# The 64 left-over rows of q and k, padded to 128 partitions and taken third in a batch, in an attention and channel-mix kernel

## The chip, the cores and the metric

The kernel runs on one core of one Trainium2 chip. The metric is the device time of one execution in microseconds (us), as the median of several runs.

## The reference

q, k and v have the shape (4, 6208, 256): four batches of N = 6208 rows with C = 256 columns. Each column of q and k is normalized over the rows, and the attention runs between columns:

```python
qn = q / (np.linalg.norm(q, axis=1, keepdims=True) + 1e-06)
kn = k / (np.linalg.norm(k, axis=1, keepdims=True) + 1e-06)
s = kn.transpose(0, 2, 1) @ qn / tau          # 256 x 256 a batch
a = softmax(s, -1)
x = v @ a                                     # 6208 x 256 a batch
```

A channel mix follows, with x_prev the row before: `xk = mu_k*x + (1-mu_k)*x_prev`, `xr` likewise with mu_r, then `relu(xk @ w_k)**2 @ w_v`, times the sigmoid of `xr @ w_r`. w_k is 256x1024, w_v 1024x256, w_r 256x256. All inputs and the output are fp32.

## The kernel before

**Tiling.** A batch's 6208 rows are NB = 12 groups of 512 and L = 64 left over. For q and k a group of 512 is a tile of 128 partitions with S = 4 rows each; the 64 left-over rows are group NB, on 64 partitions with one row each (`src`, L274). For v the tiles of 512 rows are the blocks of the main pipeline; the left-over rows of all four batches make one more block, "left", run second to last.

**Batch 0 first.** The loop at L335 loads all of batch 0's q and k (two tiles by SyncE's queue, the others by POOL's, which casts fp32 to bf16 on the way), squares them, sums the squares over the rows by matmuls with a column of ones (L376), and accumulates k^T q in PSUM, in `s_ps` (L387). `softmax(0, KC)` turns that into A[0], a 256x256 matrix in bf16 (L480). TensorE's idle time in this phase is filled with matmuls of ones (L841).

**The main pipeline.** For each block of 512 rows: `x_stage` multiplies the turned v with A (L536) and ScalarE copies the result out (L542); `mix_stage` builds xk and xr on VectorE (L576 to L599); `up_stage` multiplies with w_k (L628), with a relu on ScalarE (L632) and a square on VectorE (L634), in four pairs a block; `down_stage` multiplies with w_r (L686, the gate, tanh at L697) and w_v (L693), and VectorE joins both (L699). v is turned by TensorE for the first five blocks (L421) and by DMA transposes on SyncE's queue behind them (L409).

**Batches 1 to 3 of q and k** are worked through beside the blocks of the batch ahead. `qk_load` (L748) issues a group's two loads on POOL's queue into a ring `qk` of NG = 13 buffers; each group of a batch, the one of 64 rows too, takes the next buffer, and batch 1 begins with buffer 0, which batch 0 has used. A load's `gate` makes it wait for a pair of `up_stage`, so that loads are paced; `after_pair` (L884) names the pair, and for times ahead of the first pair it names none, so that batch 1's first two loads wait only for the buffer and for the power that `softmax(0)` takes on POOL (`root0`).

`cov_group` (L757) does a group: ScalarE squares it (L769), VectorE adds the four rows of a partition (L772, L775, in bf16) and carries the sum in fp32 in `far` (L779, L782), and TensorE adds its part of k^T q to `s_ps` (L792). With group 11 the squares in `far` are summed over the partitions by fp32 matmuls with ones (L802) into `acc` (L807). The group of 64 rows is the last of its batch: its two covariance matmuls contract over 64 partitions, its squares go into four matmuls of their own over 64 partitions (L802 again), and L809 adds the result to `acc`. Then `softmax(b)`: POOL raises the norms to the power 0.5 (L287), VectorE makes reciprocals and splits them in three bf16 terms (L289 to L308), TensorE spreads them over the partitions (L314), VectorE scales (L459), ScalarE takes exp (L473), and VectorE writes A[b] (L480).

**What sets the order.** Nothing is issued where it stands in the code. `add` notes each step with its engine, an estimated cost, its key (a due time in units of T = 9.6 us for one block) and what it reads and writes; `Plan.order` (L63) lists the steps by a model of the engines, the ready step with the smallest key first, and the program is written out in that order. Each engine runs its part in order. A step that gets another key, another cost or another buffer can so move others. The keys of a batch's groups are spaced evenly over a span (L869 to L879):

```python
span = (ends[b] - start) / 48.5
for g in range(NB + 1):
    at = start + g * S * span
    cov_group(b, g, at, span)
    need.append((at, "qk", b, g))
```

Of the kernel before, what the change touches and what calls it, by code (L numbers as in the profile page):

```python
# [174 lines left out]
def kernel(  # L175
# [17 lines left out]
    P = 128  # L193
# [14 lines left out]
    def sbuf(name, shape, dt=BF16):  # L208
        return sb.tile([P] + shape, dt, name=name)
# [125 lines left out]
    for i, (tn, g, j0, j1) in enumerate(order0):  # L335
# [43 lines left out]
        if tn == "k":  # L379
            jq = 0  # L380
            for j in range(j0, j1):
                first = "cov" not in seen
                seen.add("cov")

                def go(G=G, g=g, j=j, rows=rows, first=first):
                    for ih in range(2):
                        nc.tensor.matmul(s_ps[:, ih, :], G[:rows, 1, j, ih * P:(ih + 1) * P], G[:rows, 0, j],  # L387
                                         start=first and ih == 0, stop=False, skip_group_check=True)
                add("PE", pe(C, 2), key + .1, go, reads=[buf, ("qk", g, 0, jq)], writes=[("s_ps",)], name="cov0")
# [49 lines left out]
    LEFT = NBLK - 2  # L439


    root0 = []

    def softmax(b, key):
        i = b % 2
# [31 lines left out]
        for ih in range(2):  # L477
            add("DVE", TINY, key + .15 + .01 * ih, lambda ih=ih: nc.vector.reciprocal(sm[i][:, ih:ih + 1], sm[i][:, ih:ih + 1]),
                reads=[("sm", i, ih)], writes=[("sm", i, ih)], name="chain")
            add("DVE", dve(C, 1.4), key + .155 + .01 * ih, lambda ih=ih: nc.vector.tensor_scalar_mul(  # L480
                A[b][:, ih], e_sb[i][:, ih], sm[i][:, ih:ih + 1]), reads=[("e", i, ih), ("sm", i, ih)],
                writes=[("A", b, ih)], name="chain A")

    units = []

# [257 lines left out]
        unit(kl, both)  # L743


    ng, nl = [NB + 1], [NB + 1]

    def qk_load(b, g, key, pace):  # L748
        rows, n = (P, S) if g < NB else (L, 1)
        gi = nl[0] % NG  # L750
        nl[0] += 1
        G = qk[gi]
        for x, t in enumerate((q, k)):
            add("POOL", 0.55, key + x * .001, lambda x=x, t=t: nc.gpsimd.dma_start(G[:rows, x, :n], src(t, b, g)),  # L754
                writes=[("qk", gi, x, j) for j in range(S)], size=rows * n * C * 4, name="ld qk", after=root0, gate=pace(x))

    def cov_group(b, g, key, dk):  # L757
        rows, n = (P, S) if g < NB else (L, 1)

        def work():  # L760
            gi = ng[0] % NG
            si = ng[0] % 2
            ng[0] += 1
            G = qk[gi]
            Q = sq[si]
            both = [("qk", gi, 0, 0), ("qk", gi, 1, 0)]
            sqs = [("sq", si, 0), ("sq", si, 1)]
            w = n * 2 * C
            add("ACT", act(w), key, lambda: nc.scalar.activation(Q[:rows, :, :n], G[:rows, :, :n], AF.Square), reads=both,  # L769
                writes=sqs, name="sq")  # L770
            if n == S:
# [5 lines left out]
                F, fres = far[b % 2], ("far", b % 2)  # L777
                if g == 1:
                    add("DVE", dve(2 * C), key + .25, lambda: nc.vector.tensor_tensor(F, t2[1 - si], t2[si], op=OP.add),  # L779
                        reads=[("t2", 0), ("t2", 1)], writes=[fres], name="carry")  # L780
                elif g > 1:
                    add("DVE", dve(2 * C), key + .25, lambda: nc.vector.tensor_tensor(F, F, t2[si], op=OP.add),  # L782
                        reads=[("t2", si), fres], writes=[fres], name="carry")
                W, wres = F.rearrange("p x c -> p (x c)"), [fres]
                cols = [W[:, x * P:(x + 1) * P] for x in range(4)]
            else:
                wres = sqs
                cols = [Q[:rows, x // 2, 0, (x % 2) * P:(x % 2 + 1) * P] for x in range(4)]
            for s in range(n):
                def go(s=s):  # L790
                    for ih in range(2):
                        nc.tensor.matmul(s_ps[:, ih, :], G[:rows, 1, s, ih * P:(ih + 1) * P], G[:rows, 0, s, :],  # L792
                                         start=g == 0 and s == 0 and ih == 0, stop=g == NB and ih == 1, skip_group_check=True)
# [4 lines left out]
            one = ones_f if n == S else ones  # L798

            def go():  # L800
                for x in range(4):
                    nc.tensor.matmul(xp[:, x:x + 1], cols[x], one[:rows, 0:1], start=x == 0, stop=x == 3,  # L802
                                     skip_group_check=True)
            m_ = add("PE", (0.9, 1.05) if n == S else (0.114, 0.28), kn, go, reads=wres, take="xp", name="norm")
            ai = b % 2
            if g == NB - 1:
                add("DVE", TINY, kn - 3 * T, lambda: nc.vector.tensor_copy(acc[ai], xp[:, 0:4]), after=[m_], give="xp", writes=[("acc", ai)], name="norm")  # L807
            else:
                add("DVE", TINY, kn - 3 * T, lambda: nc.vector.tensor_tensor(acc[ai], acc[ai], xp[:, 0:4], op=OP.add),  # L809
                    after=[m_], give="xp", writes=[("acc", ai)], name="norm")  # L810
        unit(key, work)


# [136 lines left out]
```

## Time and profile before

| | |
|---|---|
| runs | 506.69, 506.70, 508.86 us; median 506.7 |
| profiled execution, its own time | 506.87 us |
| its span from first to last instruction | 505.0 us |
| granted TensorE clock | 1.000 |
| TensorE busy (matmuls) | 486.1 us, 96% |
| VectorE busy | 424.5 us, 84% |
| ScalarE busy | 408.0 us, 81% |
| POOL busy | 102.7 us, 20% |

The profile is of one execution, and the trace's times start with its first instruction. PE is TensorE's matmuls, PEld its weight loads, DVE VectorE, ACT ScalarE, POOL GpSimd, SP SyncE; L792 is line 792 of the kernel that was profiled. Matmuls are pipelined: the trace gives a start and a modelled end that reaches past the start of the next one, so that gaps between them show in the starts. Some matmul records are missing in a trace, so that a count can be one short. A row of the time line merges instructions of one line that follow each other: start, length, engine, line, operation, out<-in, shapes and count.

### The profile page before, as it was taken

Reading aid. Unit: us, or ns where it says so; the run is one execution under the profiler, and the core shown is the slowest. Engines: PE = TensorE matmul, PEld = TensorE weight load, DVE = VectorE, ACT = ScalarE, POOL = GpSimd, SP = SyncE. Lnnn points to the kernel's source line nnn. Section 1 sums busy time; section 2 is a strip of 40 time slices with the busy share of each in tenths; the row PEclk is TensorE's granted clock in tenths of the full one; section 3 lists DMA queues with packets and bytes.
Section 4 is the critical chain, followed back from the end, with each engine's and each line's share of the span. In section 5 each row is a group of like instructions: output and inputs, shape, how many; then the busy total and the mean of one; then the engine's idle time right before and its main releaser. Section 6 shows DMA issues by size and latency. Waiting matters only on the chain.

```text
span 505.0 us, 9492 instructions
## 1 busy us (share of the span) xinstructions
PE 486.1 (96%) x3477; PEld 357.3 (71%) x3536; DVE 424.5 (84%) x979; ACT 408.0 (81%) x582; POOL 102.7 (20%) x174
## 2 busy tenths in 40 slices
PE   2999999999999999999999999999999999999997
PEld 0366777777777777777776777777777777777785
DVE  4569899999899989998879999899779787878974
ACT  6867998898889888888789888888767777777774
POOL 6552222223231211222121122211110111000000
PEclk9999999999999999999999999999999999999999
DMA  9999999999999999999897999995654786542113
GB/s 209 209 205 202 152 135 162 177 228 169 214 180 143 200 180 213 180 157 179 137 176 123 185 175 160 185 169 98 142 109 84 136 123 127 103 105 63 53 75 105
DMA packets 96294, 77.36 MB, mean 153 GB/s; under 512 B 49588, under 2 KB 77944, under 8 KB 96248
## 3 DMA queue, kind: packets, MB, share of 16 engines
q0 software_dynamic: 41776, 38.84, 56.2%
q1 hardware_dynamic: 54472, 37.92, 37.5%
q8 instruction: 27, 0.44, 0.3%
q14 instruction: 19, 0.16, 0.1%
HBM read 78.71 MB, written 25.43 MB: 206 GB/s over the span
## 4 chain that ended last, share of the span: by engine, by line
PE 86%; DMA 6%; DVE 5%; issue 2%; ACT 0%; POOL 0%; DVEq 0%; ACTq 0%; POOLq 0%
PE vr L693 32%; PE kT L628 30%; PE xp L536 8%; PE vr L686 8%; PE s_ps L792 6%; DMA qk<-in_q_dram 3%; DMA v_bf<-in_v_dram 2%; DMA qk<-in_k_dram 2%; DVE kk L634 1%; DVE dl L576 1%; DVE dm L590 1%; PE kT L841 0%; ACT kr L632 0%; DVE xk L599 0%; DVE res L699 0%
## 5 line engine op out<-in xcount | busy, mean ns | idle before, releaser
L632 ACT ACTIVATE kr<-kT 128x1024 bf16<-128x1024 f32 (+1 forms) x200 | 199.7, 1001 | 51.8 <-PE kT L628 45.9
L628 PE MATMUL kT<-xk,w_k 128*128 128x512 bf16 (+1 forms) x742 | 201.2, 372 | 2.8
L693 PE MATMUL vr<-w_v,kk 128*128 128x256 bf16 x1536 | 202.2, 273 | 0.1
L634 DVE TENSOR_TENSOR kk<-kr 128x1024 bf16<-128x1024 bf16 (+1 forms) x200 | 134.1, 671 | 45.3 <-ACT kr L632 45.1
L693 PEld LDWEIGHTS <-kk 128*128 128x128 bf16 x1552 | 169.1, 112 | 3.8 <-DVE kk L634 0.4
L628 PEld LDWEIGHTS <-w_k 128*128 128x128 bf16 x800 | 77.6, 98 | 51.6 <-issue 1.5
L697 ACT ACTIVATE res<-vr 128x256 f32<-128x256 f32 x192 | 74.4, 388 | 12.2 <-PE vr L693 8.5
L699 DVE SCALAR_TENSOR_TENSOR res<-res,vr 128x256 f32<-128x256 f32 x192 | 79.4, 414 | 2.9 <-ACT res L697 2.7
L686 PE MATMUL vr<-w_r,xr 128*128 128x256 bf16 x384 | 73.4, 273 | 0.0
L769 ACT ACTIVATE sq<-qk 128x2048 bf16<-128x2048 bf16 (+1 forms) x39 | 70.6, 1811 | 2.1 <-DMA qk<-in_k_dram 1.4
L542 ACT CAST xR<-xp 128x512 bf16<-128x512 f32 x94 | 55.3, 588 | 13.5 <-PE xp L536 12.7
L403 POOL DMA_DIRECT2D v_bf<-in_v_dram x48 | 36.2, 754 | 146.1 <-PE kT L628 139.1
L686 PEld LDWEIGHTS <-xr 128*128 128x128 bf16 x384 | 42.7, 112 | 30.3 <-issue 0.2
L590 DVE TENSOR_SCALAR dm<-dl,mu 128x512 bf16<-128x512 bf16 (+1 forms) x192 | 59.0, 346 | 0.4
L536 PE MATMUL xp<-vT,A 128*128 128x512 bf16 x188 | 55.9, 379 | 0.5
L792 PE MATMUL s_ps<-qk 128*128 128x256 bf16 (+1 forms) x294 | 55.0, 273 | 0.1
L754 POOL DMA_DIRECT2D qk<-in_q_dram x39 | 20.8, 533 | 97.5 <-ACT res L697 32.4
L792 PEld LDWEIGHTS <-qk 128*128 128x128 bf16 (+1 forms) x294 | 28.5, 98 | 14.6 <-issue 0.6
L576 DVE TENSOR_TENSOR dl<-xR 128x1024 bf16<-128x1024 bf16 (+1 forms) x49 | 33.1, 676 | 0.8 <-ACT xR L542 0.6
L754 POOL DMA_DIRECT2D qk<-in_k_dram x39 | 20.8, 533 | 62.9 <-PE kT L628 42.1
L599 DVE TENSOR_TENSOR xk<-dm,xR 128x1024 bf16<-128x1024 bf16 x47 | 32.5, 691 | 0.9
L599 DVE TENSOR_TENSOR xr<-dm,xR 128x1024 bf16<-128x1024 bf16 x47 | 32.3, 687 | 0.4
(94 smaller groups left out, 259.1 us busy)
## 6 DMA issues: line engine op xcount, KB each, us to landing
out_dram<-res SPq DMA_DIRECT2D x47, 512.0 KB, 4.9
v_bf<-in_v_dram POOLq DMA_DIRECT2D x48, 256.0 KB, 6.8
qk<-in_k_dram POOLq DMA_DIRECT2D x47, 256.0 KB, 7.9
qk<-in_q_dram POOLq DMA_DIRECT2D x46, 256.0 KB, 7.7
res<-in_q_dram SPq DMA_DIRECT2D x2, 512.0 KB, 4.3
vT<-v_bf SPq DMA_TRANSPOSE x43, 7.5
w_k<-in_moe_w_k_dram POOLq DMA_DIRECT2D x1, 512.0 KB, 9.5
w_v<-in_moe_w_v_dram POOLq DMA_DIRECT2D x1, 512.0 KB, 9.5
```

What stands on the lines that cost most here:

```text
L536: nc.tensor.matmul(xp, A[b][:, ih, dh * P:(dh + 1) * P], vT[o].rearrange("p (s h) q -> p h s q", h=2)[:, ih], start=ih == 0, stop=ih == 1)
L590: unit(km, lambda col=col, dh=dh, c0=c0, c1=c1, km=km, w=w: add("DVE", dve(w, 2.77), km, lambda: nc.vector.tensor_scalar_mul(dm[di][:, dh, ...
L599: nc.vector.tensor_tensor(o[which][:, :, c0:c1], dm[di][:, :, c0:c1], xR[:, :, at + c0:at + c1], op=OP.add)
L628: last = nc.tensor.matmul(kT[bk][:, x, :w], w_k[:, dh, fh * P:(fh + 1) * P], xk[n % 2][:, dh, c0:c1], start=dh == 0, stop=dh == 1)
L632: add("ACT", act(2 * w), ku + .1, lambda: nc.scalar.activation(kr[kri][:, :, :w], kT[bk][:, :, :w], AF.Relu, scale=0.5 ** 0.5), reads=[("k ...
L634: add("DVE", dve(2 * w, 2), ku + .2, lambda: nc.vector.tensor_tensor(kk[n % 2][:, 2 * p:2 * p + 2, c0:c1], kr[kri][:, :, :w], kr[kri][:, : ...
L686: nc.tensor.matmul(V[:, D:], tokens(xr[ri][:, dh]), w_r[:, dh, :], start=dh == 0, stop=dh == 1)
L693: nc.tensor.matmul(V[:, :D], tokens(kk[n % 2][:, fh]), w_v[:, fh, :], start=fh == 0, stop=fh == 7)
L697: add("ACT", act(D), kd + .3, lambda: nc.scalar.activation(r[:, s], V[:, D:], AF.Tanh, scale=0.5), reads=[bank], writes=[("res", oi, s)], ...
L699: add("DVE", dve(D), kd + .4, lambda: nc.vector.scalar_tensor_tensor(r[:, s], r[:, s], 1.0, V[:, :D], op0=OP.add, op1=OP.mult), reads=[ban ...
L769: add("ACT", act(w), key, lambda: nc.scalar.activation(Q[:rows, :, :n], G[:rows, :, :n], AF.Square), reads=both, writes=sqs, name="sq")
L792: nc.tensor.matmul(s_ps[:, ih, :], G[:rows, 1, s, ih * P:(ih + 1) * P], G[:rows, 0, s, :], start=g == 0 and s == 0 and ih == 0, stop=g == ...
```

## The change

- The 64 left-over rows get a buffer of their own, `qkl`, with 128 partitions, whose upper 64 partitions are set to zero once, on POOL, in the head. In batches 1 to 3 their covariance matmuls contract over all 128 partitions. In batch 0 `qkl` is used too, but there the operations still take 64 partitions.
- They no longer take a buffer of the ring: a batch takes twelve, and batch 1 begins with buffer 12, which batch 0 leaves unused.
- Their squares go to `sql` on ScalarE, and VectorE adds these in fp32 to the lower 64 partitions of `far`. The four matmuls over 64 partitions and the addition to `acc` (L809) are gone; the fp32 norm matmuls cover all rows of the batch.
- In a batch the 64 rows come third, behind groups 0 and 1, in place of last. The keys' spacing goes from 1/48.5 of the batch's span to 1/49.
- A load for which `after_pair` found no pair now waits for the last VectorE step of A[0].

Lines of the changed kernel are shifted: L792 becomes L793, L802 L803, L807 L805, L536 L540, L628 L632, L693 L697; the new addition is L788.

```diff
+    qkl = sbuf("qkl", [2, 1, C])
+    sql = sbuf("sql", [2, C])
...
-        G = qk[g]
-        buf = ("qk", g, x, j0)
+        G = qk[g] if g < NB else qkl
+        buf = ("qk", g, x, j0) if g < NB else ("qkl", x)
...
+            if b == 0:
+                am.append(a_)
...
-    ng, nl = [NB + 1], [NB + 1]
+    ng, nl = [NB], [NB]
+    add("POOL", 0.4, HK + 6, lambda: nc.gpsimd.memset(qkl[L:], 0.0), writes=[("qkl0",)], name="zero")
...
-        nl[0] += 1
-        G = qk[gi]
+        nl[0] += g < NB
+        G = qk[gi] if g < NB else qkl
...
             else:
-                wres = sqs
-                cols = [Q[:rows, x // 2, 0, (x % 2) * P:(x % 2 + 1) * P] for x in range(4)]
+                G, both = qkl, [("qkl", 0), ("qkl", 1), ("qkl0",)]
+                add("ACT", act(2 * C), key, lambda: nc.scalar.activation(sql[:L], qkl[:L, :, 0], AF.Square), reads=both, writes=[("sql",)], name="sq")
+                add("DVE", dve(2 * C), key + .25, lambda: nc.vector.tensor_tensor(F[:L], F[:L], sql[:L], op=OP.add),
+                    reads=[("sql",), fres], writes=[fres], name="carry")
             for s in range(n):
                 def go(s=s):
                     for ih in range(2):
-                        nc.tensor.matmul(s_ps[:, ih, :], G[:rows, 1, s, ih * P:(ih + 1) * P], G[:rows, 0, s, :],
-                                         start=g == 0 and s == 0 and ih == 0, stop=g == NB and ih == 1, skip_group_check=True)
+                        nc.tensor.matmul(s_ps[:, ih, :], G[:, 1, s, ih * P:(ih + 1) * P], G[:, 0, s, :],
+                                         start=g == 0 and s == 0 and ih == 0, stop=g == NB - 1 and s == S - 1 and ih == 1, skip_group_check=True)
...
-            if g < NB - 1:
+            if g != NB - 1:
                 return
...
-            if g == NB - 1:
-                add("DVE", TINY, kn - 3 * T, lambda: nc.vector.tensor_copy(acc[ai], xp[:, 0:4]), after=[m_], give="xp", writes=[("acc", ai)], name="norm")
-            else:
-                add("DVE", TINY, kn - 3 * T, lambda: nc.vector.tensor_tensor(acc[ai], acc[ai], xp[:, 0:4], op=OP.add),
-                    after=[m_], give="xp", writes=[("acc", ai)], name="norm")
+            add("DVE", TINY, kn - 3 * T, lambda: nc.vector.tensor_copy(acc[b % 2], xp[:, 0:4]), after=[m_], give="xp", writes=[("acc", b % 2)], name="norm")
...
-        span = (ends[b] - start) / 48.5
-        for g in range(NB + 1):
-            at = start + g * S * span
+        span = (ends[b] - start) / 49
+        at = start
+        for g in [0, 1, NB] + list(range(2, NB)):
             cov_group(b, g, at, span)
             need.append((at, "qk", b, g))
+            at += (S if g < NB else 1) * span
...
-        return at
+        return at or am[-1:]
```

More of the change, by code (lines that the diff above doesn't have):

```diff
@@ L388, in go @@
                                          start=first and ih == 0, stop=False, skip_group_check=True)
-                add("PE", pe(C, 2), key + .1, go, reads=[buf, ("qk", g, 0, jq)], writes=[("s_ps",)], name="cov0")
+                add("PE", pe(C, 2), key + .1, go, reads=[buf, ("qk", g, 0, jq) if g < NB else ("qkl", 0)], writes=[("s_ps",)], name="cov0")
         if i == last_q:
@@ L439 @@
     LEFT = NBLK - 2
-    root0 = []
+    root0, am = [], []
     def softmax(b, key):
@@ L479, in softmax @@
                 reads=[("sm", i, ih)], writes=[("sm", i, ih)], name="chain")
-            add("DVE", dve(C, 1.4), key + .155 + .01 * ih, lambda ih=ih: nc.vector.tensor_scalar_mul(
+            a_ = add("DVE", dve(C, 1.4), key + .155 + .01 * ih, lambda ih=ih: nc.vector.tensor_scalar_mul(
                 A[b][:, ih], e_sb[i][:, ih], sm[i][:, ih:ih + 1]), reads=[("e", i, ih), ("sm", i, ih)],
                 writes=[("A", b, ih)], name="chain A")
+            if b == 0:
+                am.append(a_)
     units = []
@@ L750, in qk_load @@
         gi = nl[0] % NG
-        nl[0] += 1
-        G = qk[gi]
+        nl[0] += g < NB
+        G = qk[gi] if g < NB else qkl
         for x, t in enumerate((q, k)):
             add("POOL", 0.55, key + x * .001, lambda x=x, t=t: nc.gpsimd.dma_start(G[:rows, x, :n], src(t, b, g)),
-                writes=[("qk", gi, x, j) for j in range(S)], size=rows * n * C * 4, name="ld qk", after=root0, gate=pace(x))
+                writes=[("qk", gi, x, j) for j in range(S)] if g < NB else [("qkl", x)], size=rows * n * C * 4, name="ld qk", after=root0, gate=pace(x))
     def cov_group(b, g, key, dk):
@@ L760, in work @@
         def work():
[L761 to L771, printed above, removed]
+            gi, si = ng[0] % NG, ng[0] % 2
+            F, fres = far[b % 2], ("far", b % 2)
+            if g < NB:
+                ng[0] += 1
+                G, Q = qk[gi], sq[si]
+                both = [("qk", gi, 0, 0), ("qk", gi, 1, 0)]
+                sqs = [("sq", si, 0), ("sq", si, 1)]
+                add("ACT", act(n * 2 * C), key, lambda: nc.scalar.activation(Q, G, AF.Square), reads=both, writes=sqs, name="sq")
                 add("DVE", dve(2 * 2 * C, 2), key + .1, lambda: nc.vector.tensor_tensor(
@@ L776, in work @@
                     reads=[("t1", si)], writes=[("t2", si)], name="sum")
-                F, fres = far[b % 2], ("far", b % 2)
                 if g == 1:
```

10 lines of the change are left out of this document (3 added, 7 removed).

## The prediction

> **What bounds the kernel now.** I read the profile's first line, then busy time by stage, then TensorE's own waits, then the order of its instructions around the 64-row groups.
>
> ```profile
> span 505.0 us, 9492 instructions
> ```
> ```profile
> 0.00:38.70 38.70, 26.83 (x199) 14.26 (x200) 22.35 (x72) 27.29 (x32) 23.07 (x44) 1.00 1.09 207
> 38.70:49.00 10.30, 10.06 (x82) 7.26 (x83) 9.60 (x26) 7.13 (x14) 2.56 (x4) 1.00 1.31 204
> 49.00:499.00 450.00, 446.71 (x3177) 333.80 (x3233) 390.93 (x879) 372.77 (x534) 77.05 (x126) 1.00 0.93 148
> 65.00:80.00 15.00, 14.89 (x112) 11.23 (x112) 14.88 (x33) 14.33 (x18) 3.62 (x6) 1.00 1.23 140
> ```
>
> Each row has the stretch, its length, then busy us and instructions of TensorE, its weight loads, VectorE (DVE), ScalarE (ACT) and POOL, the granted clock, the DMA share and GB/s. Until 38.7 us the kernel loads q and k of batch 0 (207 GB/s) up to the first matmul with A; from 38.7 to 49 VectorE is as full as TensorE (9.60 of 10.30); from 49 to 499 TensorE is busy 446.71 of 450 us at clock 1.00. The longest entry among all that TensorE's matmuls waited for (us in total, times, longest):
>
> ```profile
> PE vr L376 <- DVE t L364: 10.3, 5, 7.3
> ```
>
> L376 is batch 0's own norm line, so it lies in the head. Behind 49 us TensorE waits for nothing of that size: the time there is the sum of its instructions, and only what shortens that sum, or breaks its density, moves the end.
>
> Busy time hides one thing, because a matmul's modelled end overlaps the next start. Starts show it. TensorE around the first batch's 64 rows (start, us, line, count), and then the same places in the last:
>
> ```profile
> 138.18 1.04 PE L693 MATMUL vr<-w_v,kk 128*128 128x256 bf16 x8
> 139.15 0.39 PE L792 MATMUL s_ps<-qk 64*128 64x256 bf16 x2
> 139.47 1.04 PE L628 MATMUL kT<-xk,w_k 128*128 128x512 bf16 x3
> ...
> 141.00 1.04 PE L693 MATMUL vr<-w_v,kk 128*128 128x256 bf16 x8
> 141.87 1.03 PE L628 MATMUL kT<-xk,w_k 128*128 128x512 bf16 x4
> ...
> 143.98 0.38 PE L693 MATMUL vr<-w_v,kk 128*128 128x256 bf16 x2
> 144.29 0.25 PE L802 MATMUL xp<-ones,sq 64*128 64x1 bf16 x4
> 144.47 0.85 PE L693 MATMUL vr<-w_v,kk 128*128 128x256 bf16 x6
> ```
> ```profile
> 370.40 0.39 PE L792 MATMUL s_ps<-qk 64*128 64x256 bf16 x2
> 370.72 0.60 PE L628 MATMUL kT<-xk,w_k 128*128 128x512 bf16 x2
> ...
> 374.89 0.25 PE L802 MATMUL xp<-ones,sq 64*128 64x1 bf16 x4
> 375.07 0.41 PE L686 MATMUL vr<-w_r,xr 128*128 128x256 bf16 x2
> ```
>
> Undisturbed, eight 256-column matmuls take 141.87 - 141.00 = 0.87 us, 0.109 each. The eight from 138.18 would end at 139.05, but the two 64-row matmuls start at 139.15; these should be done at 139.37, but L628 starts at 139.47: **0.10 us lost on the way into 64 rows and 0.10 on the way out**. In the last batch 370.72 - 370.40 = 0.32 against 0.22 gives the same 0.10 on the way out. The four norm matmuls over 64 rows: L693 is through at 143.98 + 0.22 = 144.20, the next full matmul starts at 144.47, so 0.27 us go for them and their two changes. In the last batch they take 375.07 - 374.89 = 0.18 from start to start, without the way in: 0.28 with 0.10 for it.
>
> **The change part by part.** All terms are against the profiled execution, 506.87 us: its span of 505.0 and 1.87 around it. The median of the runs shown, 506.7, lies 0.17 under that.
>
> *Covariance over 128 rows, three times.* Two matmuls of 256 columns remain.
>
> ```profile
> L792 PE MATMUL s_ps<-qk x294: 269/273/280, 55.7 to 370.5; 128*128 128x256 bf16 x144, 64*128 64x256 bf16 x3
> ```
>
> Shortest and longest over both shapes lie 11 ns apart, so zeros in the upper 64 rows cost no time of their own. The two changes go: -0.20 us a batch, -0.60 in all.
>
> *Norm matmuls over 64 rows gone.* Four matmuls and two changes, 0.27 and 0.28 us by the rows above: -0.28 a batch, -0.84 in all. The eight fp32 norm matmuls stay.
>
> The loss at each change fits a rule of the Trainium skill, "TensorEngine Tiling (Array Packing)", section Tiling Modes: changing the tiling mode drains the array. "TensorE: Matmul & The Clock Gate", on the steps of a matmul, gives the drain as some 128 cycles, by which the twelve changes would be an estimated 0.64 us; the rows show about 0.10 each, some 1.2, and they decide.
>
> *VectorE.* Three additions of 64x512 in fp32 come, three of four numbers go.
>
> ```profile
> L782 DVE TENSOR_TENSOR far<-far,t 128x512 f32<-128x512 f32 x30 | 20.6, 688 | 0.6
> L809 DVE TENSOR_TENSOR acc<-acc,xp 128x4 f32<-128x4 f32 x3 | 0.5, 155 | 1.5 <-PE xp L802 1.5
> ```
>
> The nearest row has the same free size, 0.69 us; that makes 3 x (0.69 - 0.16) = 1.6 us more work, ahead of the end only where VectorE holds TensorE up. Behind 49 us it has 450 - 391 = 59 us to spare. I take 0. The cover is thin in one place, 65 to 80 us, where VectorE is busy 14.88 of 15 and ScalarE 14.33: batch 1's 64-row square (some 0.6 us on ScalarE, moved here from near 139 us) and its addition now fall there. Both uncovered: +1.3 at most.
>
> *The memset of qkl and the moved xR memset,* on POOL's queue ahead of three q loads:
>
> ```profile
> 3.49 0.26 POOL masks.py:197 MEMSET ident<- 128x128 bf16 x1
> ...
> 7.42 0.53 POOL L350 DMA_DIRECT2D qk<-in_q_dram  x1 [0.80 <-DMA qk<-in_q_dram]
> ```
>
> 128 columns take 0.26 us, so qkl's 512 take between that and four times it, 1.04. The three loads behind it go out that much later; the queue then idles 0.80 us for a landing before 7.42 anyhow, and the loads already out keep the DMA engines working meanwhile. I take 0, ends 0 and 1.04 - 0.80 = +0.24.
>
> *First loads of batch 1 wait for A.*
>
> ```profile
> 36.69 0.58 POOL L754 DMA_DIRECT2D qk<-in_q_dram  x1
> 37.27 0.54 POOL L754 DMA_DIRECT2D qk<-in_k_dram  x1
> 37.80 0.76 POOL L403 DMA_DIRECT2D v_bf<-in_v_dram  x1
> 42.32 0.54 POOL L754 DMA_DIRECT2D qk<-in_q_dram  x1 [3.77 <-PE kT L628]
> ```
> ```profile
> 38.77 0.35 DVE L480 TENSOR_SCALAR A<-e_sb,sm 128x256 bf16<-128x256 f32 x1
> ```
> ```profile
> v_bf<-in_v_dram POOLq DMA_DIRECT2D x48, 256.0 KB, 6.8
> qk<-in_k_dram POOLq DMA_DIRECT2D x47, 256.0 KB, 7.9
> ```
> ```profile
> 53.75 0.61 PE L421 MATMUL kT<-ident,v_bf 128*128 128x128 bf16 x8
> ...
> 55.72 1.04 PE L792 MATMUL s_ps<-qk 128*128 128x256 bf16 x8
> ```
>
> A is done at 39.12. The q and k loads and the v load queued behind them on POOL go out from 39.15 to 41.0 instead of 36.69 to 38.56, and are through before the next issue at 42.32, so nothing further back is moved. They land near 39.7 + 7.9 = 47.6 and 40.3 + 6.8 = 47.1; their first uses are at 55.72 and 53.75. Six us of slack hide it, and I take 0. The other end is a gain: the weights and v tiles ahead in the queue no longer share 207 GB/s with them. But the stage to 49 us hangs on VectorE, so I see no use for it; -0.24, all that TensorE stands idle in that stage (10.30 less 10.06), is the bound.
>
> *Group order and buffers.* The 64 rows' two loads move in POOL's queue, their squares in ScalarE's and their covariance in TensorE's from last to third in a batch, and a batch takes twelve of the thirteen buffers in place of thirteen. Every count stays. SP's DMAs keep their number; two pairs change places. In the built order the small loads have 11.5 us of matmul time from the release of the k load to its use, counted with 0.109 and 0.215 us a matmul; the same count for the nearest group of before is 12.6. The norm sum now has one matmul step less behind it; that chain is off the path, as it was. I take 0.
>
> **Sum:** 506.87 - 0.60 - 0.84 = 505.43; set to the median, -0.17: **505.3 us**.
>
> **The rivals.** *VectorE or ScalarE becomes the bound* at 65 to 80 us: +0.3 to +1.3, so 505.6 to 506.6. For it: 14.88 of 15. Against it: TensorE there loses nothing today. *The padding doesn't remove the loss:* if the 0.20 around the covariance came from the other buffer and not from the rows, 0.60 comes back: 505.9. Against it: the idle comes at the norm matmuls too, which read another buffer.
>
> *Slower:* the softmax hand-over. POOL raises the norms to a power behind whatever load stands ahead in its queue, and the order there has changed.
>
> ```profile
> 258.53 0.53 POOL L754 DMA_DIRECT2D qk<-in_q_dram  x1 [2.25 <-issue]
> ```
> ```profile
> 382.70 0.63 DVE L480 TENSOR_SCALAR A<-e_sb,sm 128x256 bf16<-128x256 f32 x2
> ```
> ```profile
> 383.68 0.59 PE xp L536 x2
> ```
>
> A load ahead of the power waited 2.25 us at 258.53. A is ready at 383.33 and first used at 383.68: slack 0.35. A load that held the power back by 2.25 beyond today's start would stop TensorE for 1.9 us a batch, 5.7 in all, and give 511.0; from a delay of 0.35 + 0.48 a batch on, the kernel is slower than before. Against it: in the built order the gates of the loads ahead of the power open before the norm matmuls in all three batches, and from the end of the spread to the first use of A stand 3.9, 4.3 and 3.9 us of matmuls (before: 5.0, 3.9, 3.7).
>
> *Faster yet:* the head gains its 0.24 us from the held-back loads: 505.0.
>
> **How the numbers follow.** Forecast, 505.1 to 505.6: 0.57. VectorE or ScalarE: 0.18. Loss remains: 0.07. Slower: 0.09. Faster yet: 0.09. The range reaches from 504.5 (the head's 0.24 and half a microsecond of waits too short to be listed, of the 450 - 446.7 us) to 507.6, the unknown costs uncovered together (+1.3, +0.24) and 0.8 of one hand-over's stall; that leaves out most of the slower case and the tail of the faster. A measurement of this kernel tells 0.5% (2.5 us) from no change; faster by more than that 0.03, within 0.88, slower 0.09.
>
> **What would show it.** Right: no 64-row shape at the changed lines of batches 1 to 3; the starts around the padded covariance follow at 0.109 and 0.215; the 64x1 matmuls are gone; TensorE behind 49 us waits for nothing new; the first use of A stays near 38.7 and the stage to 49 keeps its length. Wrong: gaps of 0.1 around a 128-row covariance; a wait of L693 for kk at 65 to 80 us; a wait of L540 for A after a spread; a first load landing after its use.

## The result, and the profile after

| | before | after |
|---|---|---|
| median of 22 runs each | 506.83 us (506.52 to 508.94) | 504.86 us (504.6 to 508.47) |
| profiled execution | 506.87 us, span 505.0 | 504.73 us, span 503.0 |

The ratio after to before is **0.9961, 95% interval 0.995 to 0.9973**: 2.0 us faster. The forecast was 505.3, the range 504.5 to 507.6. Single runs of every kernel, before included, come out up to some 7 us above its shortest (one, of the kernel with its own norm matmuls below, took 644.76 us), so an experiment is given by its median and, in brackets, its shortest run. The experiments ran in three groups on three chips, where before gave medians of 506.94, 507.78 and 507.06 us and an unchanged copy of the changed kernel 505.66; a difference under some 1 us between kernels is therefore read from the shortest runs and from the starts, not from the medians.

Busy time by stage in the changed kernel, in the columns of the rows shown for before:

```profile
38.70:49.00 10.30, 9.97 (x83) 7.15 (x81) 9.52 (x25) 7.29 (x15) 4.42 (x7) 1.00 1.31 204
49.00:499.00 450.00, 449.98 (x3240) 335.90 (x3240) 392.88 (x881) 371.49 (x536) 77.67 (x126) 1.00 0.92 148
65.00:80.00 15.00, 15.00 (x109) 11.11 (x107) 14.69 (x32) 12.91 (x19) 3.39 (x6) 1.00 1.22 172
```

The stage to 49 us is as it was, with TensorE idle 0.33 us of 10.30 against 0.24. Behind 49 us TensorE is now busy 449.98 of 450 us. The 3.3 us more than before are mostly not a gain: the trace of before has 3177 matmul records there for 3233 weight loads, this one 3240 for 3240, and where a record is missing a part of its time counts as idle. A second profile of the same changed kernel, with 3180 records, shows as little as before:

```profile
49.00:499.00 450.00, 446.90 (x3180) 335.60 (x3236) 392.65 (x880) 371.51 (x536) 77.64 (x126) 1.00 0.92 148
```

What was gained must be read from the starts. Between 65 and 80 us VectorE and ScalarE have more room than they had (14.69 and 12.91 us against 14.88 and 14.33): the first batch's 64-row square on ScalarE ends at 65.0, just ahead of that stretch, and VectorE's addition at 66.5 fits in.

TensorE's order around the padded 64 rows of the first batch, and around its norms:

```profile
62.37 1.03 PE L632 MATMUL kT<-xk,w_k 128*128 128x512 bf16 x4
63.24 0.38 PE L793 MATMUL s_ps<-qkl 128*128 128x256 bf16 x2
63.45 0.55 PE L423 MATMUL kT<-ident,v_bf 128*128 128x128 bf16 x7
...
142.25 0.95 PE L803 MATMUL xp<-ones_f,far 128*128 128x1 f32 x8
143.06 0.38 PE L793 MATMUL s_ps<-qk 128*128 128x256 bf16 x2
```

Four matmuls of 512 columns at 0.215 end at 62.37 + 0.86 = 63.23, and the two for the 64 rows start at 63.24; 63.24 + 0.22 = 63.46, and the next starts at 63.45. No gap is left on either side. The 64x1 matmuls are gone; eight fp32 ones fill 0.81 us.

Where the 2.0 us come from is read from two marks, the first matmul with A on TensorE's time line and the last store on that of SyncE's queue (SPq). Before:

```profile
38.74 0.28 PE L513 MATMUL kT<-vT,A 128*128 128x256 bf16 x1
```
```profile
502.06 0.40 SPq L715 DMA_DIRECT2D out_dram<-res  x1
```

After:

```profile
38.45 0.27 PE L517 MATMUL kT<-vT,A 128*128 128x256 bf16 x1
```
```profile
500.05 0.40 SPq L719 DMA_DIRECT2D out_dram<-res  x1
```

The head is 38.74 - 38.45 = 0.29 us shorter. The **middle**, from mark to mark, goes from 463.32 to 461.60: 1.72 less. The forecast had 1.44 of it. The other 0.28 is, to 0.01, a wait in the second batch of before that the prediction did not list, because it is too short to stand out. TensorE and its weight loads there:

```profile
264.56 1.04 PE L792 MATMUL s_ps<-qk 128*128 128x256 bf16 x8
265.70 0.39 PE L628 MATMUL kT<-xk,w_k 128*128 128x512 bf16 x1
```
```profile
265.70 0.11 PEld L628 LDWEIGHTS <-w_k 128*128 128x128 bf16 x2 [0.38 <-DVE xk L599]
```

Eight matmuls from 264.56 end at 265.43, and L628 starts at 265.70, 0.27 us later, held up by VectorE's xk. In the changed kernel the matmuls around that time follow each other without a gap:

```profile
264.43 0.38 PE L690 MATMUL vr<-w_r,xr 128*128 128x256 bf16 x2
264.65 0.93 PE L697 MATMUL vr<-w_v,kk 128*128 128x256 bf16 x7
```

Only one gap of 0.1 us is left behind 50 us in this profile, in the spread of batch 1 ahead of 148.48. The second profile of the same kernel has two others, 0.10 us at 139.3 and 0.25 at 179.8, and a middle of 461.97: gaps of this size come and go from one execution to the next.

### The profile page after: what moved, and what is told of

It reads as the page before. It is cut to its first block, busy times and chain, and to the rows that moved or that the text cites. A ratio compares the mean times of both kernels' runs of the same rounds, so it can differ in the third digit from the quotient of the medians.

```text
span 503.0 us, 9519 instructions
## 1 busy us (share of the span) xinstructions
PE 486.4 (97%) x3524; PEld 357.1 (71%) x3524; DVE 426.1 (85%) x979; ACT 405.9 (81%) x582; POOL 104.2 (21%) x175
## 4 chain that ended last, share of the span: by engine, by line
PE 90%; DMA 6%; DVE 2%; issue 0%; POOL 0%; ACT 0%; POOLq 0%
PE vr L697 33%; PE kT L632 33%; PE vr L690 8%; PE xp L540 8%; PE s_ps L793 6%; DMA qk<-in_q_dram 3%; DMA qk<-in_k_dram 2%; DMA v_bf<-in_v_dram 2%; PE xp L803 0%; PE kT L836 0%; DVE kk L638 0%; DVE xk L588 0%; PE kT L697 0%; DVE xr L588 0%; POOL qk L352 0%
## 5 line engine op out<-in xcount | busy, mean ns | idle before, releaser
L632 PE MATMUL kT<-xk,w_k 128*128 128x512 bf16 (+1 forms) x800 | 207.0, 373 | 0.2
L697 PE MATMUL vr<-w_v,kk 128*128 128x256 bf16 x1536 | 202.8, 273 | 0.0
L697 PEld LDWEIGHTS <-kk 128*128 128x128 bf16 x1552 | 169.3, 112 | 4.9 <-DVE kk L638 0.2
L632 PEld LDWEIGHTS <-w_k 128*128 128x128 bf16 x800 | 77.8, 98 | 49.7 <-issue 0.9
L773 ACT ACTIVATE sq<-qk 128x2048 bf16<-128x2048 bf16 x36 | 68.8, 1910 | 0.0
L540 PE MATMUL xp<-vT,A 128*128 128x512 bf16 x188 | 55.9, 379 | 0.0
L793 PE MATMUL s_ps<-qk 128*128 128x256 bf16 x288 | 54.0, 273 | 0.0
L793 PEld LDWEIGHTS <-qk 128*128 128x128 bf16 x288 | 28.2, 98 | 16.1
L774 DVE TENSOR_TENSOR t<-sq 128x1024 bf16<-128x1024 bf16 x36 | 24.8, 688 | 12.5 <-ACT sq L773 12.5
L759 POOL DMA_DIRECT2D qk<-in_q_dram x36 | 19.4, 538 | 73.3 <-PE kT L632 17.5
```

Of the source, the lines that this page charges most:

```text
L540: nc.tensor.matmul(xp, A[b][:, ih, dh * P:(dh + 1) * P], vT[o].rearrange("p (s h) q -> p h s q", h=2)[:, ih], start=ih == 0, stop=ih == 1)
L632: last = nc.tensor.matmul(kT[bk][:, x, :w], w_k[:, dh, fh * P:(fh + 1) * P], xk[n % 2][:, dh, c0:c1], start=dh == 0, stop=dh == 1)
L697: nc.tensor.matmul(V[:, :D], tokens(kk[n % 2][:, fh]), w_v[:, fh, :], start=fh == 0, stop=fh == 7)
L773: add("ACT", act(n * 2 * C), key, lambda: nc.scalar.activation(Q, G, AF.Square), reads=both, writes=sqs, name="sq")
L793: nc.tensor.matmul(s_ps[:, ih, :], G[:, 1, s, ih * P:(ih + 1) * P], G[:, 0, s, :], start=g == 0 and s == 0 and ih == 0, stop=g == NB - 1 a ...
```

## The experiments

The theory was that of the prediction: TensorE's order is the bound, a change between 64 and 128 rows costs 0.10 us each way, the norm matmuls their own time on top, and the remaining edits cost nothing. The rivals: that the cost comes from any partial tile, that the place of the 64 rows or the hold of the first loads does the work, or that the head does. Each ratio is to the kernel before on the same chip.

### Covariance over 64 rows again

```diff
-  G[:, 1, s, ih * P:(ih + 1) * P], G[:, 0, s, :]
+  G[:rows, 1, s, ih * P:(ih + 1) * P], G[:rows, 0, s, :]
```

> The changed kernel, but the covariance of the 64 rows in batches 1 to 3 contracts over 64 partitions again, out of the same buffer qkl. Theory (each change between 128 and 64 rows costs TensorE 0.10 us): six changes come back, +0.60 us against the changed kernel's 504.86, so 505.5, and gaps of 0.10 ahead of and behind the two matmuls. Rival (the loss came from the other buffer or the place in the order): +0.0, 504.9, and no gaps.

Measured: 505.71 us (shortest 505.18), ratio 0.9968, interval 0.9949 to 0.9987. TensorE around the first batch's 64 rows:

```profile
62.30 1.03 PE L632 MATMUL kT<-xk,w_k 128*128 128x512 bf16 x4
63.26 0.39 PE L793 MATMUL s_ps<-qkl 64*128 64x256 bf16 x2
63.58 0.62 PE L423 MATMUL kT<-ident,v_bf 128*128 128x128 bf16 x8
```

62.30 + 0.86 = 63.16, start at 63.26; 63.26 + 0.22 = 63.48, next start at 63.58. The 0.10 on each side is back, in the new buffer and at the new place, so it belongs to the rows and not to the buffer. That settles where the price lies. Its size in the total is less firm: the shortest run is 0.58 above the 504.6 of the changed kernel, where 0.60 was reckoned, but the ratio to before (0.9968) is not told apart from that of the changed kernel (0.9961). The profile is of the longest of the eleven runs, 506.77 us; by the starts it has stalls of 0.28, 0.30 and 0.79 us elsewhere, ahead of 125.7, 153.4 and 156.15.

### Own norm matmuls over 64 rows again, third in line

The squares of the 64 rows are not added to `far`; they go through four matmuls over 64 partitions and L809's addition to `acc`, as before, but third in the batch.

```diff
-                add("DVE", dve(2 * C), key + .25, lambda: nc.vector.tensor_tensor(F[:L], F[:L], sql[:L], op=OP.add),
-                    reads=[("sql",), fres], writes=[fres], name="carry")
...
-            W = F.rearrange("p x c -> p (x c)")
+            W = F.rearrange("p x c -> p (x c)") if g < NB else sql[:L].rearrange("p x c -> p (x c)")
+            one, wres = (ones_f, [fres]) if g < NB else (ones[:L, 0:1], [("sql",)])
```

> The changed kernel, but the squares of the 64 rows are summed by four matmuls of their own over 64 partitions, third in line, and added to acc, as before the change; the covariance stays padded. Theory: three visits of 0.27 to 0.28 us come back, +0.84, so 505.7. Rival (the small matmuls stood beside other waits and their removal was worth nothing; what counted was the shorter way to the softmax): at most +0.2, 505.1.

Measured: 506.08 us (505.76), ratio 0.998, interval 0.9957 to 1.0003. The visit in the first batch:

```profile
66.92 0.38 PE L697 MATMUL vr<-w_v,kk 128*128 128x256 bf16 x2
67.23 0.25 PE L802 MATMUL xp<-ones,sql 64*128 64x1 bf16 x4
67.41 0.60 PE L632 MATMUL kT<-xk,w_k 128*128 128x512 bf16 x2
```

66.92 + 0.22 = 67.14, start at 67.23, next full matmul at 67.41: 0.27 us, as before. The shortest run is 1.16 above that of the changed kernel, 0.32 more than three such visits. The stores show where: compared with the changed kernel they fall back by 0.53 us in the first batch, then by 0.33 and 0.31. In the first batch two more gaps of 0.07 and 0.15 us follow, ahead of 68.80 and 70.25. The visit is right in size; this arrangement loses a little more beside it.

### The padding alone, in the kernel before

Before, with `qkl` and its zeros, covariance and the own norm matmuls over 128 rows, the 64 rows still last and without the hold.

> The kernel before, with one thing of the change: the 64 rows sit in a zeroed buffer of 128 partitions, and both their covariance and their four norm matmuls run over 128 partitions; they stay last in line, the norm matmuls and the addition to acc stay. Theory: all twelve changes go, the four small matmuls (0.03 each at least) stay: -0.60 - 3 x (0.28 - 0.12) = -1.1 us against 506.83, so 505.7. Rival (it is the removal of the small matmuls and the place third in line that pay): 0 to -0.6.

Measured: 506.43 us (506.12), ratio 0.9997, interval 0.9982 to 1.0013. Its first batch:

```profile
139.14 0.38 PE L794 MATMUL s_ps<-qkl 128*128 128x256 bf16 x2
139.36 1.03 PE L629 MATMUL kT<-xk,w_k 128*128 128x512 bf16 x4
...
144.10 0.24 PE L804 MATMUL xp<-ones,sq 128*128 128x1 bf16 x4
144.20 0.83 PE L694 MATMUL vr<-w_v,kk 128*128 128x256 bf16 x6
```

The starts around both visits follow without a gap, and the norm visit costs 0.10 us in place of 0.28: the 1.1 us that were expected are there, place by place. Yet the middle is only 462.51, 0.81 less than before, and the median falls by 0.5. Part of the difference is a longer wait for xk:

```profile
265.38 0.60 PE L629 MATMUL kT<-xk,w_k 128*128 128x512 bf16 x2 [0.30 <-DVE xk L600]
```

By its starts this stall is 0.46 us in place of 0.27; gaps of 0.06 and 0.12 us stand ahead of 149.27 and 149.73. Removing a gap ahead of a wait only lets TensorE arrive earlier at the wait. So the miss in this run is not in the price of a tile change, but in my taking it for granted that what is saved reaches the end.

### Without the hold, twice

```diff
-        return at or am[-1:]
+        return at
```

> The changed kernel, but batch 1's first two loads don't wait for A. Theory A (the hold is worth nothing; the stage up to 49 us hangs on VectorE): 504.9. Theory B (the 0.3 us by which the first matmul with A comes earlier in the changed kernel, 38.45 against 38.74, is the hold's): +0.3, 505.2, with the first matmul with A back near 38.7.

Measured: 508.37 us (504.87 to 512.27), ratio 1.0024, interval 0.9989 to 1.0059. Neither theory had this. So it was run again, beside an unchanged copy of the changed kernel:

> The changed kernel without the hold of the first loads of batch 1, a second time: the first time gave a median of 508.37 us with single runs from 504.87 to 512.27, and a profile in which TensorE waited for a load of k at 82.15. Theory A, the hold matters: without it the loads of batch 1 come in another rhythm and TensorE waits for one at 80 to 90 us; median 507 to 508.5, scattered again, while the unchanged kernel of this group stays at 504.9. Theory B, the chip or its memory was disturbed in that run: 504.9 to 505.2, no wait of TensorE for a load of k between 60 and 100 us.

> The changed kernel once more, unchanged, beside the three others of this group: 504.9 us by every theory (the median on record is 504.86). It is the mark against which the others of the group are read.

Measured: without the hold 506.95 us (505.03 to 509.0), ratio 0.9996, interval 0.9981 to 1.0011; unchanged 505.66 us (504.75 to 508.93), ratio 0.9973, interval 0.9952 to 0.9994. The shortest run is some 0.3 above that of the changed kernel both times, the median 1.3 on the same chip, and in the first run more. The intervals of the second pair overlap, so 1.3 is no exact price; but neither time is the kernel without the hold told apart from before. The second time theory A's 507 to 508.5 was nearly met, but without the wait for a load of k that it named; theory B's time was not met, nor the copy's 504.9. In the profiles the loss is new waits, at another place each time. First run, the two longest, 0.40 and 0.93 us by the starts:

```profile
82.15 0.39 PE L793 MATMUL s_ps<-qk 128*128 128x256 bf16 x2 [0.24 <-DMA qk<-in_k_dram]
...
89.54 0.82 PE L632 MATMUL kT<-xk,w_k 128*128 128x512 bf16 x3 [0.77 <-DVE xk L603]
```

Second run, the longest, 1.57 us by the starts:

```profile
156.13 0.59 PE L540 MATMUL xp<-vT,A 128*128 128x512 bf16 x2 [1.41 <-ACT xR L546]
```

Such a wait is not the mark of a missing hold: the profile with the covariance over 64 rows has the hold, and its 0.79 us ahead of 156.15 are the same wait for xR. So the runs show longer medians without the hold, and not which wait it prevents.

How long a load of q or k takes from its issue to its landing between 60 and 95 us (shortest, median, longest), in the changed kernel:

```profile
DMA to landing us min/median/max: 4.5/7.0/8.8
```

and in the first and the second run without the hold:

```profile
DMA to landing us min/median/max: 9.6/11.3/13.1
```
```profile
DMA to landing us min/median/max: 8.1/9.3/11.3
```

A hold that ends at 39 us cannot delay or hasten a load at 70 us by itself. What differs in between is the **written order**. The planner counts the hold in its model of the engines and places the third held load's use, eight transposing matmuls of v, later. With the hold (changed kernel), those matmuls on TensorE, and SyncE's first store:

```profile
56.28 0.61 PE L423 MATMUL kT<-ident,v_bf 128*128 128x128 bf16 x8
```
```profile
57.34 0.43 SPq L717 DMA_DIRECT2D out_dram<-res  x1
```

and without it (first run):

```profile
54.14 0.61 PE L423 MATMUL kT<-ident,v_bf 128*128 128x128 bf16 x8
```
```profile
60.64 0.43 SPq L717 DMA_DIRECT2D out_dram<-res  x1
```

The first block's output is finished and stored 3 us earlier with the hold, and the DMA transposes queued behind that store on SyncE start earlier too, at 57.81 against 61.11. In all nine profiles with the hold the first store goes out at 57.3 to 57.5, in all five without it at 60.1 to 61.2. That the earlier store and transposes make the later loads land sooner fits, also with the kernel before (median 11.0 us) and the hold alone in it (7.6). But no run changes that order without the hold, and one kernel speaks against it as the only cause: the padding alone has no hold, stores at 60.34, and its loads land in 6.0 us all the same.

### The hold alone, in the kernel before

```diff
-        return at
+        return at or am[-1:]
```

> The kernel before, with one thing of the change: batch 1's first two loads wait for A. Theory A (the hold is worth nothing): 506.8. Theory B (the hold gives the head's 0.3 us): 506.5, and the first matmul with A near 38.45.

Measured: 507.38 us (506.65), ratio 0.9989, interval 0.9971 to 1.0007. The middle is 463.31, the 463.32 of before to a hundredth; only the head differs, by 0.17 us. Here the new order is there too (first store at 57.45) and gives nothing. So the hold is no gain by itself; whatever it is worth, it is worth only together with the rest of the change.

### The zeros alone, in the kernel before

The memset of `qkl` on POOL, and nothing that reads it.

> The kernel before with one thing added, the zeros written over the upper 64 partitions of qkl at the head (nothing reads them). Theory A, what moves the start of the first matmul with A from 38.7 to 38.5 us is the code at the head (the memset on GpSimd's queue): first such matmul at 38.45, time 506.5. Theory B, the memset lies hidden and that start belongs to the hold or to chance: first such matmul at 38.7 to 39.1, time 506.8. In both the six changes of the tile size stay, and the stall near 265 us of 0.27 to 0.3.

Measured: 508.39 us (506.85), ratio 1.0027, interval 1.0005 to 1.0049. Neither theory: the first matmul with A comes at 39.69. The memset takes 0.52 us there, as in the changed kernel:

```profile
4.69 0.52 POOL L748 MEMSET qkl<- 64x512 bf16 x1
5.16 1.70 POOL L351 DMA_DIRECT2D qk<-in_q_dram  x3
8.22 0.59 POOL L351 DMA_DIRECT2D qk<-in_q_dram  x1 [1.36 <-DMA qk<-in_q_dram]
```

In before the row after the wait stands at 7.42, so this head runs 0.8 us late from its ninth load on; the shortest run, though, is only 0.28 us above that of before, near the 0.24 that the prediction had as its bound. In the changed kernel the memset stands at the same 4.69, but that load follows at 7.34, and A is early. The first matmul with A, over all kernels, follows the moment at which POOL takes the power, by 2.4 to 2.7 us; that moment hangs on when the last loads of the head land, and it spreads from 35.76 to 36.99. The five profiles without the hold mostly come later (first matmul at 38.59 to 39.69, with the hold 38.34 to 38.62), but there the power is mostly late already, ahead of the instruction that the hold delays. In all fourteen profiles the power follows the landing of batch 0's last load of k by 1.25 to 1.29 us. That load, issued at 26.55 before and 26.57 after, lands at 34.74 and 34.48: 0.26 of the 0.29. But in the two profiles of the one kernel without the hold it lands at 35.12 and 34.62, and A is first used at 39.11 and 38.59, a spread of 0.5 us with one program. **So the head's 0.29 us may be scatter of that landing; whether the change has a part in it stays open.**

### One slice of every group over 64 and over 96 rows

In the changed kernel one of the four covariance slices of each of the 36 groups of 512 contracts over 64 partitions; the upper 64 rows of that slice are left out of k^T q. In the second kernel it is 96 partitions, and the upper 32 rows are left out.

```diff
-  G[:, 1, s, ih * P:(ih + 1) * P], G[:, 0, s, :]
+  G[:64 if s == 1 else P, 1, s, ih * P:(ih + 1) * P], G[:64 if s == 1 else P, 0, s, :]
```

> The changed kernel, but in each of the 36 full groups of batches 1 to 3 the second of the four slices is multiplied over its lower 64 partitions alone; the rows on the upper 64 of that slice are left out of the covariance. 36 visits to 64 rows more, 72 changes, and not one matmul more. Theory (0.10 us a change): +7.2 us, 512.1. Rival (a contraction over 64 rows costs what one over 128 does, and the gaps of before were waits of that place): 504.9.

> As the kernel with 64 rows in the second slice, but with 96 of 128 partitions; the upper 32 are left out. If the loss comes from a change of the array's tile (64 rows make a smaller tile, 96 don't), +0, 504.9. If any change of the number of rows drains the array: +7.2 us, 512.1.

Measured over 64 rows: **512.42 us** (512.29 to 512.58), ratio 1.0082, interval 1.0051 to 1.0114. Over 96 rows: **505.13 us** (504.87), ratio 0.9962, interval 0.9938 to 0.9987. Over 64 rows:

```profile
97.31 1.04 PE L697 MATMUL vr<-w_v,kk 128*128 128x256 bf16 x8
98.28 0.39 PE L793 MATMUL s_ps<-qk 64*128 64x256 bf16 x2
98.60 0.60 PE L632 MATMUL kT<-xk,w_k 128*128 128x512 bf16 x2
```

Over 96 rows:

```profile
96.76 0.38 PE L793 MATMUL s_ps<-qk 96*128 96x256 bf16 x2
96.98 0.60 PE L632 MATMUL kT<-xk,w_k 128*128 128x512 bf16 x2
```

97.31 + 0.87 = 98.18 against 98.28, and 98.28 + 0.22 = 98.50 against 98.60; with 96 rows the next start comes after 0.22. 36 visits at 0.20 are 7.2 us; 512.42 less 504.86 is 7.6. This is the cleanest result of the study: the price belongs to 64 rows, not to any number of rows below 128. The Trainium skill, "TensorEngine Tiling (Array Packing)", section Tiling Modes, lists row tilings of 128, 64 and 32 rows and says that a change of the tiling mode drains TensorE; there is no mode of 96 rows in the list, and the run agrees: 96 rows cost no change.

### The 64 rows second to last

```diff
-        for g in [0, 1, NB] + list(range(2, NB)):
+        for g in list(range(NB - 1)) + [NB, NB - 1]:
```

> The changed kernel, but the 64 rows come second to last in a batch, ahead of group 11, in place of third. Theory (the place is worth nothing, the sum of TensorE's instructions is the same): 504.9, within 0.3. Rival (third in line takes work away from the crowded end of a batch): 0.5 to 1.5 us more.

Measured: 505.76 us (505.39), ratio 0.9957, interval 0.9941 to 0.9973; the shortest run is 0.79 above that of the changed kernel. The spread of batch 1's norms:

```profile
147.37 0.38 PE L793 MATMUL s_ps<-qk 128*128 128x256 bf16 x2
147.59 0.42 PE L316 MATMUL xp<-ident,rb 128*128 128x128 bf16 x2
148.44 0.40 PE L316 MATMUL xp<-ident,rb 128*128 128x128 bf16 x4 [0.43 <-DVE rb L310]
```

Two matmuls of 128 columns are through 0.11 us after 147.59, and the next starts at 148.44: a stall of 0.74, the three bf16 terms on VectorE being late. With 0.16 more at 154.29 that is what this kernel loses. By the shortest runs and the profiles third in line is worth some 0.8 us against second to last, as the rival had it; the ratios to before, 0.9957 here and 0.9961, do not show it. In this profile the loss lies in the softmax hand-over of one batch: the power on POOL starts at 143.77 in both kernels, but takes 2.01 us here and 1.48 in the changed kernel, and VectorE idles 0.93 us for it. Why it takes longer is not known.

### Norm matmuls in bf16

The last addition to a batch's sum of squares writes bf16, so that each partition's sum is rounded once more, and the norm matmuls take bf16 in place of fp32. `O` is the bf16 tile `farb` in the last group and `F` in the others.

```diff
-  tensor_tensor(F, F, t2[si], op=OP.add)
+  tensor_tensor(O, F, t2[si], op=OP.add)
...
-            W = F.rearrange("p x c -> p (x c)")
+            W = farb[b % 2].rearrange("p x c -> p (x c)")
...
-  xp[:, x:x + 1], W[:, x * P:(x + 1) * P], ones_f
+  xp[:, x:x + 1], W[:, x * P:(x + 1) * P], ones[:, 0:1]
```

> The changed kernel, with the last sum of the squares written in bf16 and the norm matmuls run on bf16 instead of fp32 (the norms are then rounded to bf16 once before they are summed). In the profile of the changed kernel eight fp32 norm matmuls take 0.95 us and start a batch's norm 0.79 to 0.81 us ahead of what follows. Theory A, TensorE's order is the bound and fp32 costs several passes: four matmuls of 128x1 in bf16 take 0.12 to 0.25 us a batch, so three times 0.55 to 0.67 come off: 502.9 to 503.2. Theory B, the time of a norm is that of its four weight loads or of its wait for VectorE's sum and not of the data type: 504.9.

Measured: **503.55 us** (503.36), ratio 0.9934, interval 0.9913 to 0.9954: faster than both kernels, by 2.1 us against the unchanged copy on the same chip in the median and 1.4 in the shortest run. Its first batch's norm on TensorE, and then the weight loads of that norm, here and in the changed kernel:

```profile
142.34 0.24 PE L805 MATMUL xp<-ones,farb 128*128 128x1 bf16 x4
142.45 0.38 PE L795 MATMUL s_ps<-qk 128*128 128x256 bf16 x2
```
```profile
142.13 0.37 PEld L805 LDWEIGHTS <-farb 128*128 128x128 bf16 x4
```
```profile
142.03 1.08 PEld L803 LDWEIGHTS xp<-ones_f,far 128*128 128x128 f32 x8
```

From the norm's start to what follows it are 0.11 us, against 0.81 in the changed kernel: 0.70 a batch, a little more than theory A had. Four matmuls of one column show eight weight loads and eight matmul records in fp32, and four of each in bf16, and the matmuls start at the pace of the loads. So I read the time of a norm as that of its weights, as theory B did, but it does hang on the data type. The run changes the type of both operands at once, so that this reading is argued and not isolated. The Trainium skill, "TensorE: Matmul & The Clock Gate", section "Weight-path perf modes — Fast Weight Load (FWL) and DoubleRow", says that the fast weight load is on for 128 weights whose type is not fp32; the trace agrees, with 0.11 us from one fp32 load to the next and some 0.03 in bf16. By the stores, measured against the changed kernel, the first batch brings 0.58, the third 0.69, and the second only 0.07. There the earlier norm arrives at the softmax hand-over, as its weight loads show:

```profile
260.53 0.10 PEld L317 LDWEIGHTS <-rb 128*128 128x128 bf16 x1 [0.25 <-DVE rb L310]
260.86 0.23 PEld L317 LDWEIGHTS <-rb 128*128 128x128 bf16 x4 [0.23 <-DVE rb L311]
264.82 0.10 PEld L541 LDWEIGHTS <-A 128*128 128x128 bf16 x1 [0.47 <-DVE A L483]
```

TensorE waits for the split norms and for A, which did not come as much earlier. VectorE had written acc at 256.02, but on POOL the power stood behind a load of q that waited for its gate:

```profile
256.20 0.53 POOL L760 DMA_DIRECT2D qk<-in_q_dram  x1 [1.44 <-ACT kr L637]
256.75 1.40 POOL L290 TENSOR_TENSOR nrm<-acc,half 128x4 f32<-128x4 f32 x1
```

So some 1.35 of the three times 0.70 us, 2.1, reach the end, and 503.55 stays above theory A's 502.9 to 503.2.

## Why the prediction was right, point by point

- **Covariance over 128 rows, -0.60: right.** Starts after the change follow without a gap. That the zeros cost nothing the prediction took from modelled lengths; the starts show it, with 0.22 us for the two padded matmuls. Put back, the gaps of 0.10 us come back, and 0.58 us between the shortest runs; the price is that of 64 rows, as 64 against 96 rows shows.
- **Norm matmuls over 64 rows gone, -0.84: right in size.** Put back, a visit takes 0.27 us. That kernel lost 1.16 in all, the other 0.32 to small gaps beside the visits, which was not reckoned.
- **VectorE and ScalarE at no cost: right.** TensorE lost nothing at 65 to 80 us, nor behind 80.
- **Memset at no cost: right in this kernel, in its size between the ends** (0.52 us, ends 0.26 and 1.04). Alone in the kernel before it was not free in that profile, so its cover is thin.
- **The head: missed by 0.29 us.** The prediction took 38.7 for the first use of A to stay, and let the head gain only as a rival, through VectorE's stage to 49 us. The gain lies ahead of 38.7, where the last load of batch 0 landed 0.26 us sooner; two profiles of one kernel differ by more, so that it may be scatter.
- **The middle: 1.72 in place of 1.44.** The other 0.28 us is the wait for xk at 265.70 in the second batch. The prediction took 450 - 446.7 us behind 49 us for time in which TensorE waits, and used that for the lower end of the range; most of it is missing matmul records, since the copy of the changed kernel shows 446.90 too. The wait for xk stays in all four kernels on the order of before (0.27 us, 0.46 with the padding, 0.28 with the hold, 0.27 with the zeros), and none of the others has it, whether they keep the hold or not and whether the 64 rows are third or second to last. So it went with the rest of the new order; which part of that took it away was not tried.
- **"Nothing further back is moved" by the hold: wrong.** The argument followed the loads on POOL's queue, and there it holds. But a wait counts in the planner's model, and the planner moved eight matmuls of v and, with them, the first store and the transposes by 3 us. Without the hold the changed kernel gives 506.95 and 508.37. The forecast came out all the same, because the kernel has the hold.
- **Group order at no cost: right as put, and not idle.** Third in line cost nothing; second to last costs 0.8 us at a hand-over in its profile.
- **The slower rival: a late hand-over does stop TensorE, but not in this kernel.** It shows where the norms run in bf16, with 0.25 to 0.35 us a stall and the power behind a load, as the prediction had it; and where the 64 rows are taken second to last, with 0.74 us, but there the power waits for acc alone and no load holds it up. No stall of 1.9 us came.

Added up against the profiled execution: 506.87 less 1.44 gave 505.43, and 504.73 came. The other 0.70 are 0.29 of the head, 0.28 of the middle (the wait for xk), and 0.14 outside the span (1.87 us before, 1.73 after), to the rounding. The middle without that wait fell by some 1.45 us, as forecast; undone one at a time the two terms give more, 0.58 and 1.16, since each gap that is put back shifts other waits.

The median of 504.86 lies 0.24 below the stretch from 505.1 to 505.6 that the prediction held likeliest, and inside the range by its lower end. That end was set for a gain of the head behind 38.7 and for half a microsecond of short waits, read from time that is mostly missing records. The first did not come, and of the second one wait of 0.27 us was real. The two terms of the sum were understood; that the extra gain stayed inside the range is partly luck.

## What to carry to other kernels

Where TensorE is dense, read the starts and not the busy time: a small operation on 64 rows pays its tile change twice, and zeros in the other rows cost nothing if they are written once. Read no gain from a busy share without comparing the numbers of records. An fp32 matmul of one column here went at the pace of its weight loads, so the type of the weights is the first thing to look at. And where a planner writes the order, a new wait or a new cost is two edits, the wait and another order: compare the written orders before calling either free, and ask of each saving which wait TensorE then reaches earlier.

## What the runs showed of the hardware that was not expected

- A contraction over 96 rows has no price among matmuls over 128 (36 visits, 505.13 us); one over 64 rows has 0.10 us on each side (36 visits, 512.42 us).
- Fp32 weights of 128x128 take 0.11 us from one load to the next, with two loads a matmul, bf16 ones some 0.03 with one, and a norm of four fp32 matmuls costs 0.81 us and one of four bf16 matmuls 0.11.
- The same loads, issued at about the same times, land after 7.0 us in the median in one kernel and after 11.3 in another that differs in the written order around 57 us; what decides it was not isolated.
